# Transposing the columns of a recurrent step by DMA instead of by TensorE, and a softmax moved ahead, in a fused two-layer kernel

## The chip, the cores and the metric

The kernel runs on one core of a Trainium2 chip. The metric is the device time of one execution in microseconds (us), lower being better. Times shown are medians of several executions; a profile is one further execution with the hardware profiler on.

## What is computed

Two identical layers work on x, 2048 tokens of 448 values, in bf16. Each layer adds an attention part and then a gated feed-forward part.

```
x = x + A(layernorm(x));  x = x + B(layernorm(x))      # layer 1
x = x + A(layernorm(x));  x = x + B(layernorm(x))      # layer 2

A: mem = mem0                                   # 8 tokens
   for s in range(64):                          # segments of 32 tokens
       h = concat(mem, x[32s : 32s+32])         # 40 tokens
       q, k, v = h Wq, h Wk, h Wv               # 16 heads of 256
       p = softmax(mask(q k^T / 16))            # a token sees the 8 memory tokens and the tokens up to itself
       o = (p v) Wo
       mem, out[s] = o[:8], o[8:]               # the memory goes to the next segment
B: (relu(x Wgate) * (x Wup)) Wdown              # 448 -> 1792 -> 448
```

The loop over segments is a recurrence: segment s+1 can't begin until the 8 memory rows of segment s are there.

## The kernel before

**Folded weights.** At the start the kernel multiplies Wq with Wk^T and Wv with Wo for every head, so that a step needs neither keys nor values: scores come from h and a projected h (`A_sb`), and the output from the weighted rows of h itself, multiplied by `B_sb`. Heads are handled in two halves, called half 0 and half 1 (`hf`).

**Steps.** The main loop (line 1148) has 68 steps. Step g works on segment g of layer 1 and on segment g - 4 of layer 2 at once, so steps 4 to 63 have two layers ("two-layer steps", `two`), the first and last four have one. Every odd step from g = 3 on also carries a block of feed-forward work, `ff` (lines 545 to 682). I call these *long steps*, and the even ones *short steps*. In the two-layer stretch short and long steps alternate, 30 of each.

**A step's data.** The step's tokens stand as columns in `hT` (`hb[:, j, :]`): 448 features on partitions, in four chunks of 128 columns. VectorE and ScalarE write the new tokens' columns in `rows_in` (line 299, from the long step before), and VectorE writes the memory columns at the very end of the step before, in `project_last` (line 959) and in `finish` (line 967, the copy `hT<-ox`). The output needs the same tokens as rows too: 128 token slots on partitions, features along. This is `hk`, one of two buffers `HK[g % 2]` (line 525).

**How `hk` is made before.** `hk_make` (line 831) multiplies each of the four chunks of `hb` with the identity on TensorE, into one PSUM bank `kps`, and ScalarE copies that into `hk` in two pieces. `hk` is first read in `weigh_m(0, ...)`, then by `weigh_m(1, ...)` and `weigh_x`.

**Order within a step** (`step`, line 813). TensorE's instructions run in the order of the program text (`in_order`, line 84), and so do those of VectorE, ScalarE and of the DMA queue SP (`InOrder`, line 97). A step begins with `project(0, ...)`: half 0 of the projected h (`prj`), in five banks; after the second one `hk_make` stands. In long steps the residual and layer norm of the feed-forward block run on VectorE meanwhile, and `ff.fetch()` transposes the normed tokens (`xn`) into `xT`. Then `late` runs: `weigh_x(1, ...)` of the step before, which needs that step's half-1 weights `px1`. Then come half 1's projections, the scores of memory rows (`Sm`) and of ordinary rows (`Sx`), their softmaxes, and the output products (`ox`, `o`) by `project_out` and `project_last`.

**A softmax** (line 759) is four closures: `[3]` adds the mask, `[0]` takes the peak and subtracts it (VectorE), `[1]` is the exponential (ScalarE), `[2]` is sum, reciprocal and product (VectorE), which leaves the weights in `PX` (ordinary rows) or `PM` (memory rows). `m0`, `m1`, `x0`, `x1` are the softmaxes of memory and ordinary rows of half 0 and 1.

**How weights become columns.** Two ways exist. `flipped` transposes on TensorE (`pps`) and copies to `PT`. `fetched` (line 805) goes by DMA: SP writes `PX` to a scratch in DRAM (`dx`) and reads it back with a transposing DMA into `PT`; both are issued one after the other:

```
119  def turned(out, src, tag):
121      d = dram.tile([src.shape[0], src.shape[1]], BF, tag=f"d{tag}", name=f"d{tag}")
122      sp.dma_start(d[:], src)
123      sp.dma_start_transpose(out, d[:])
```

In two-layer steps a long step fetches `px0` and `px1`; a short step flips `px0` and fetches `px1` near its end. The read waits for the write to land, and whatever stands behind it on SP waits with it. `px1` is used by `weigh_x(1, ...)` early in the following step.

**SP's queue** in a pair of two-layer steps, before: short step `dx`, `PT` (half 1); long step `dxn`, `xT`, `dx`, `PT` (half 0), `dx`, `PT` (half 1), then four transfers of tokens (`xa<-xp`, `out_dram<-xa`, `xa<-in_A_x_dram`, `xp<-in_A_x_dram`).

Of the kernel before, what the change touches and what calls it, by code (L numbers as in the profile page):

```python
# [8 lines left out]
BF = mybir.dt.bfloat16  # L9
# [6 lines left out]
DM = 448  # L16
# [15 lines left out]
HI = 128  # L32
HW = 4 * HI
# [30 lines left out]
def build_kernel(ctx, tc, A_x, A_mem0, A_Wq, A_Wk, A_Wv, A_Wo, B_W_gate, B_W_up, B_W_down, out,  # L64
                 ntiles=16, nseg=64):
    nc = tc.nc
    P = nc.NUM_PARTITIONS
# [12 lines left out]
    dram = ctx.enter_context(tc.tile_pool(name="dram", bufs=2, space=bass.MemoryType.DRAM))  # L80
# [35 lines left out]

    dve, act, sp = InOrder(nc.vector), InOrder(nc.scalar), InOrder(nc.sync)

    def turned(out, src, tag):

        d = dram.tile([src.shape[0], src.shape[1]], BF, tag=f"d{tag}", name=f"d{tag}")
        sp.dma_start(d[:], src)
        sp.dma_start_transpose(out, d[:])

    now = [0]
    free_at = [0] * 8
# [3 lines left out]
    def bank(shape, dtype, name, after=700, hold=False):  # L130

        i = min((i for i in range(8) if i not in held), key=lambda i: free_at[i])
        t = psum.tile(shape, dtype, tag=f"b{i}", name=name)
        bank_of[t.name] = (i, after)
        free_at[i] = now[0] + 1000
        if hold:
            held.add(i)
        return t
# [25 lines left out]
    def evac(eng, dst, src):  # L164
        if eng is act:
            act.copy(dst, src)
        else:
            eng.tensor_copy(dst, src)
# [356 lines left out]
    HK = []  # L525
# [188 lines left out]
    def project(hf, chains, hb, j, banks, pre={}, busy=False, first=None, inside=None, head=0, between=None):  # L714

        n = L * len(chains)
        for i0, k in banks:
            ps = pre[i0] if i0 in pre else bank([P, 512], F32, "prj")
            two = len(chains) == 2

            def copies(eng, rows, T):
                if two:
                    evac(eng, T, ps[rows, 0:k * n].rearrange("p (t g q) -> p t g q", t=k, q=16))
                    return
                c = chains[0]
                src = ps[rows, 0:k * n].rearrange("p (t w) -> p t w", t=k)
                x, m = (0, SEG) if c == 0 else (MEM, 0)
                evac(eng, T[:, :, 2, MEM * c:MEM * c + MEM], src[:, :, m:m + MEM])
                evac(eng, T[:, :, 3 * c:3 * c + 2, :],
                     src[:, :, x:x + SEG].rearrange("p t (g q) -> p t g q", q=16))  # L730

            for i in range(k):
                if inside is not None and i == 4:
                    inside()
                if i0 not in pre:
                    tile_of(ps, hf, i0 + i, i, chains, hb, j, range(4), True, True)
                elif i >= head or i0 != banks[0][0]:
                    tile_of(ps, hf, i0 + i, i, chains, hb, j, range(3), False, True)
            if i0 in pre:
                let_go(ps)  # L740
            if first is not None:
                first()
            if between is not None:
                between()
            if i0 < 24:
                u0, eo = i0 // 12 * 6, i0 // 6 % 2
                T = TQ[hf][:].rearrange("p g u w -> p g (u w)").rearrange("p g (t e q) -> p t e g q", e=2, q=16)
                T = T[:, u0:u0 + 6, eo]
                copies(act if (i0 != 6 if busy and hf else i0 % 12) else dve, slice(0, P), T)
            else:  # L750
                for eng, e in ((act if busy else dve, 0), (act, 1)):
                    copies(eng, FR[e], TZ[hf][FR[e]].rearrange("p g (t e q) -> p t e g q", e=2, q=16)[:, :, e])
            if i0 in (6, 18):
                next_piece()
# [49 lines left out]

    def fetched(src, tag):
        PT = main.tile([P, 2, 128], BF, tag=f"PT{tag}", name="PT")
        turned(PT[:], src[:].rearrange("p b w -> p (b w)"), tag)
        return PT[:].rearrange("p b q -> p (b q)")

    def active(g):  # L810
# [2 lines left out]
    def step(g, ff, pre, late):  # L813
# [3 lines left out]
        gb, j = divmod(g, BLK)  # L817
        hb = hTb[gb % 2]
# [12 lines left out]
        def hk_make():  # L831
            kps = bank([P, 4, 128], F32, "kps")
            for i in range(4):
                n = 128 if i < 3 else 64
                mm(kps[:, i, 0:n], hb[:, j, i * HI:(i + 1) * HI], ident[:, 0:n], start=True, stop=True)
            hk = HK[g % 2]
            evac(act, hk[:].rearrange("p k n -> p (k n)")[:, 0:DM],
                 kps[:].rearrange("p k n -> p (k n)")[:, 0:DM])
            act.copy(hk[:, 4, 64:128], kps[:, 3, 0:64])
            return hk  # L840
# [46 lines left out]
        def weigh_m(hf, hk, PT):  # L887
            if not ms:
                return
            ya = bank([P, 256], F32, "ya")  # L890
            for kd in range(2):
                mm(ya[:, kd * 128:kd * 128 + 128], hk[:, kd, :], PT[:], start=True, stop=True)
            dve.tensor_copy(YB[hf][:, 0:16, M0:M0 + 16], ya[:].rearrange("p (t q) -> p t q", q=16))
            yb = bank([P, 192], F32, "yb")
            mm(yb[:, 0:128], hk[:, 2, :], PT[:], start=True, stop=True)
            for eo in range(2):
                mm(yb[:, 128:192], hk[:, 3 + eo, :], PT[:].rearrange("p (b o q) -> p b o q", o=2, q=16)[:, :, eo, :], start=(eo == 0), stop=(eo == 1))
            act.copy(YB[hf][:, 16:28, M0:M0 + 16], yb[:].rearrange("p (t q) -> p t q", q=16))
# [78 lines left out]
        def feed(*us):  # L977
            if ff is not None:
                for u in us:
                    ff.gate_up(u)  # L980


        two = len(chains) == 2
        early = ff is not None and two
        project(0, chains, hb, j, BANKS[0][0:1], pre, between=ff.residual if early else None)
        project(0, chains, hb, j, BANKS[0][1:2], pre)
        hk = hk_make()
        if ff is not None and not two:
            ff.residual()
        next_piece()  # L990
# [47 lines left out]
        m1, x1 = scores(1, True, True)  # L1038
# [24 lines left out]
        if ff is not None:  # L1063
            x1[3]()
            if len(chains) == 1:
                x0[0]()
                x1[0]()
            ox_open()
            mid = 18 if two else 10
            project_out(0, 0, mid)  # L1070
            ff.open_rows((0, 1, 2))
            if len(chains) == 2:
                x0[0]()
            x0[1]()
            m1[2]()
            x0[2]()
            if two:
                px0 = fetched(PX[0], "x0")
            feed(0)
            next_piece()  # L1080
            if len(chains) == 2:
                x1[0]()
            ff.products(1)
            ff.gated(1)
            pm = flipped(PM[1], 1, "m1", act) if ms else None
            x1[1]()
            ff.products(2)
            x1[2]()
            if two:
                px1 = fetched(PX[1], "x1")  # L1090
            else:
                px0 = flipped(PX[0], 2, "x0", act)
            weigh_m(1, hk, pm)
            ff.gated(2)
            feed(3)
            project_out(0, mid, mid + 8)
            next_piece()
            ff.down()
            ff.norm2()
            project_out(0, mid + 8, NT)  # L1100
            project_last()
            next_piece()
            project_out(1, 0, 12)
            if not two:
                px1 = flipped(PX[1], 2, "x1")
            fed = 20 if two else 18
            project_out(1, 12, fed)
            ff.feed_on()
            project_out(1, fed, NT)
        else:  # L1110
            next_piece()
            ox_open()
            m1[2]()
            x0[0]()
            x0[1]()
            late_flip = 23
            project_out(0, 0, late_flip)
            pm = flipped(PM[1], 1, "m1") if ms else None
            project_out(0, late_flip, NT)
            weigh_m(1, hk, pm)  # L1120
            x0[2]()
            x1[3]()
            x1[0]()
            x1[1]()
            x1[2]()
            if two:
                px1 = fetched(PX[1], "x1")
            next_piece()
            project_last()
            project_out(1, 0, 10)  # L1130
            px0 = flipped(PX[0], 2, "x0", act)
            project_out(1, 10, 25)
            if not two:
                px1 = flipped(PX[1], 2, "x1", act)
            next_piece()
            project_out(1, 25, NT)
# [11 lines left out]
    for g in range(nsteps):  # L1148
# [5 lines left out]
        i = (g - 3) // 2  # L1154
# [88 lines left out]
```

## Time and profile before

| | us |
|---|---|
| median of 3 runs | 1547.64 (1546.91 to 1550.41) |
| profiled execution, its own time | 1552.72 |
| span of the profile | 1550.9 |
| one short step, in the middle (801.20 to 818.95) | 17.75 |
| the long step after it (818.95 to 845.49) | 26.54 |
| copies `hk<-kps` on ScalarE, mean of one | 0.539 and 0.232 |
| writes `dx<-PX` and reads `PT<-dx` on SP | 90 of each |

In a line of the profile, L153 is the helper through which every matmul goes and L106 the one through which VectorE, ScalarE and SP go, so instructions are told apart by the names of their tiles. Names stand as output<-input. PE is TensorE's matmul, PEld its weight load, DVE VectorE, ACT ScalarE, POOL GpSimd, and SPq the queue SP on which DMAs are issued; the time in an SPq line is that of issuing, and a DMA's landing is listed apart. A timeline line has start, busy time, engine, instruction and, in brackets, the idle time before it and what ended that. Neighbouring matmuls overlap, so a group of them costs the distance from its start to the next group's start.

### The profile page before, as it was taken

Reading aid. Unit: us, or ns where it says so; the run is one execution under the profiler, and the core shown is the slowest. Engines: PE = TensorE matmul, PEld = TensorE weight load, DVE = VectorE, ACT = ScalarE, POOL = GpSimd, SP = SyncE. Lnnn points to the kernel's source line nnn. Section 1 sums busy time; section 2 is a strip of 40 time slices with the busy share of each in tenths; the row PEclk is TensorE's granted clock in tenths of the full one; section 3 lists DMA queues with packets and bytes.
Section 4 is the critical chain, followed back from the end, with each engine's and each line's share of the span. In section 5 each row is a group of like instructions: output and inputs, shape, how many; then the busy total and the mean of one; then the engine's idle time right before and its main releaser. Section 6 shows DMA issues by size and latency. Waiting matters only on the chain.

```text
span 1550.9 us, 89067 instructions
## 1 busy us (share of the span) xinstructions
PE 1533.7 (99%) x40635; PEld 1423.9 (92%) x40635; DVE 1092.4 (70%) x3591; ACT 744.3 (48%) x2059; POOL 77.6 (5%) x173
## 2 busy tenths in 40 slices
PE   9999999999999999999999999999999999999998
PEld 6689999999999999998999999999999999999997
DVE  7756777777777777776677777776767777767765
ACT  6744444454444444544454445444544544445444
POOL 3200000000000000000000000000000000000000
PEclk9999999999999999999999999999999999999999
DMA  8620011100100111000011101000011001000000
GB/s 254 204 65 11 20 27 26 25 22 22 25 20 23 27 26 25 22 22 24 18 25 27 26 21 23 24 22 23 24 27 27 21 22 25 20 22 24 23 7 10
DMA packets 88393, 52.22 MB, mean 34 GB/s; under 512 B 48008, under 2 KB 87120, under 8 KB 88016
## 3 DMA queue, kind: packets, MB, share of 16 engines
q1 hardware_dynamic: 85888, 42.33, 10.4%
q8 instruction: 318, 5.21, 1.4%
q0 software_dynamic: 1088, 3.68, 0.7%
q10 hardware_dynamic: 1040, 0.52, 0.1%
q14 instruction: 59, 0.48, 0.1%
HBM read 23.18 MB, written 11.60 MB: 22 GB/s over the span
## 4 chain that ended last, share of the span: by engine, by line
PE 96%; DMA 2%; DVE 1%; issue 0%; ACT 0%; POOL 0%; SPq 0%; DVEq 0%; ACTq 0%; POOLq 0%
PE prj L153 31%; PE ox L153 25%; PE gps L153 6%; PE ups L153 6%; PE dps L153 6%; PE o L153 5%; PE y L153 4%; PE Sx L153 3%; PE bps L153 1%; PE Sm L153 1%; PE ya L153 1%; PE aps L153 1%; PE yb L153 1%; PE tpw L161 1%; PE kps L153 1%; PE pps L161 1%
## 5 line engine op out<-in xcount | busy, mean ns | idle before, releaser
L153 PE MATMUL prj<-hT,A_sb 128*128 128x80 bf16 (+3 forms) x15232 | 551.8, 199 | 1.0 <-issue 0.6
L153 PEld LDWEIGHTS <-A_sb 128*128 128x128 bf16 (+1 forms) x15232 | 505.5, 99 | 21.2 <-issue 1.4
L153 PEld LDWEIGHTS <-B_sb 128*128 128x128 bf16 (+1 forms) x15008 | 484.7, 103 | 15.4 <-issue 2.4
L153 PE MATMUL ox<-Y,B_sb 128*128 128x80 bf16 (+2 forms) x11256 | 436.3, 200 | 1.9 <-issue 1.7
L106 ACT CAST TQ<-prj 128x480 bf16<-128x480 f32 (+1 forms) x380 | 184.5, 498 | 100.9 <-PE prj L153 87.7
L106 DVE CAST Y<-y 128x256 bf16<-128x256 f32 x376 | 151.3, 458 | 48.6 <-PE y L153 46.4
L106 ACT CAST Y<-y 128x512 bf16<-128x512 f32 (+2 forms) x392 | 137.0, 419 | 99.5 <-PE y L153 94.1
L106 ACT ACTIVATE se<-se 128x160 f32<-128x160 f32 (+2 forms) x270 | 81.6, 302 | 184.6 <-DVE se L106 176.1
L106 DVE CAST TQ<-prj 128x480 bf16<-128x480 f32 (+1 forms) x228 | 127.8, 569 | 15.7 <-PE prj L153 15.2
L153 PE MATMUL gps<-xT,Wg_sb 128*128 128x128 bf16 (+3 forms) x1904 | 128.7, 215 | 0.0
L106 DVE SCALAR_TENSOR_TENSOR hh<-gps,ut 128x512 bf16<-128x512 f32 (+2 forms) x136 | 78.1, 595 | 60.9 <-PE gps L153 37.8
L153 PEld LDWEIGHTS <-Wu_sb 128*128 128x128 bf16 (+1 forms) x1904 | 105.0, 97 | 5.7 <-issue 0.2
L153 PEld LDWEIGHTS <-hk 40*128 40x128 bf16 (+1 forms) x1950 | 98.8, 96 | 12.2 <-DMA PT<-dx 4.9
L153 PE MATMUL ups<-xT,Wu_sb 128*128 128x128 bf16 (+3 forms) x1632 | 107.0, 216 | 1.6 <-DMA xT<-dxn 1.2
L153 PEld LDWEIGHTS <-Wg_sb 128*128 128x128 bf16 (+1 forms) x1904 | 106.8, 97 | 1.6 <-issue 1.5
L106 DVE TENSOR_REDUCE ssum<-se 128x4 f32<-128x160 f32 (+2 forms) x270 | 73.4, 272 | 42.3 <-ACT se L106 38.5
L106 ACT CAST TZ<-prj 64x320 bf16<-64x320 f32 (+2 forms) x264 | 96.9, 377 | 8.4 <-DVE TZ L106 5.3
L106 ACT CAST ut<-ups 128x512 bf16<-128x512 f32 (+1 forms) x102 | 57.4, 563 | 81.1 <-PE ups L153 81.1
L106 ACT COPY os<-o 64x16 f32<-64x16 f32 (+3 forms) x134 | 25.6, 191 | 146.1 <-PE o L153 144.5
L153 PE MATMUL dps<-Wd_sb,hh 128*128 128x448 bf16 (+1 forms) x504 | 93.3, 342 | 0.8 <-DVE hh L106 0.8
L153 PE MATMUL y<-PT,hk 40*128 40x256 bf16 (+1 forms) x1280 | 86.0, 248 | 4.3 <-DMA PT<-dx 4.1
L106 DVE CAST Y<-ya 128x256 bf16<-128x256 f32 x134 | 56.9, 425 | 47.0 <-PE ya L153 46.5
(138 smaller groups left out, 1801.0 us busy)
## 6 DMA issues: line engine op xcount, KB each, us to landing
dx<-PX SPq DMA_DIRECT2D x90, 64.0 KB, 1.5
dxn<-xn SPq DMA_DIRECT2D x29, 128.0 KB, 1.7
wo<-in_A_Wo_dram POOLq DMA_DIRECT2D x8, 448.0 KB, 5.2
nat<-in_A_Wv_dram SPq DMA_DIRECT2D x8, 384.0 KB, 4.8
nat<-in_A_Wq_dram SPq DMA_DIRECT2D x6, 384.0 KB, 4.3
nat<-in_A_Wk_dram SPq DMA_DIRECT2D x6, 384.0 KB, 4.9
xa<-in_A_x_dram SPq DMA_DIRECT2D x32, 56.0 KB, 2.5
xa<-xp SPq DMA_DIRECT2D x32, 56.0 KB, 1.9
```

The costliest lines, as they stand in the source:

```text
L106: r = f(*a, **k)
L153: in_order(nc.tensor.matmul(out, lhsT, rhs, **k))
L161: in_order(nc.tensor.transpose(out, src, idn))
```

## The change

Two things change, both in two-layer steps only.

*The columns become rows by DMA.* At the head of the step, SP writes the step's columns (128 partitions, four chunks of 128) to a DRAM scratch `dh` of 512 rows of 128 values, one row for each feature, and two transposing DMAs read 448 and 64 of these rows into `hk`. The four matmuls into `kps` and ScalarE's two copies go away in these steps; one-layer steps keep `hk_make`. So that SP issues `dh` ahead of it, the transposing read of a fetched `PX` is no longer issued by `fetched` itself but kept in a list `to_read`, and issued by `read_rest`: in long steps at once, after a short step at the head of the next step, behind `dh`.

*Half 1's softmax of ordinary rows moves up in short steps.* The mask's addition `x1[3]` goes ahead of the first part of `project_out(0, ...)`, and peak, subtraction and exponential ahead of `x0[2]`, half 0's sum and product.

```diff
+    to_read = []
+
+    def sent(src, tag):
         d = dram.tile([src.shape[0], src.shape[1]], BF, tag=f"d{tag}", name=f"d{tag}")
         sp.dma_start(d[:], src)
-        sp.dma_start_transpose(out, d[:])
+        return d
+
+    def turned(out, src, tag):
+        sp.dma_start_transpose(out, sent(src, tag)[:])
+
+    def read_rest():
+        while to_read:
+            sp.dma_start_transpose(*to_read.pop(0))
...
     def fetched(src, tag):
         PT = main.tile([P, 2, 128], BF, tag=f"PT{tag}", name="PT")
-        turned(PT[:], src[:].rearrange("p b w -> p (b w)"), tag)
+        to_read.append((PT[:], sent(src[:].rearrange("p b w -> p (b w)"), tag)[:]))
...
         two = len(chains) == 2
         early = ff is not None and two
+        if two:
+            rows = dram.tile([HW, HI], BF, tag="dh", name="dh")
+            sp.dma_start(rows[:].rearrange("(i p) q -> p i q", p=P), hb[:, j, :].rearrange("p (i q) -> p i q", q=HI))
+        read_rest()
+        if two:
+            hk = HK[g % 2]
+            flat = hk[:].rearrange("p k n -> p (k n)")
+            sp.dma_start_transpose(flat[:, 0:DM].unsqueeze(1), rows[0:DM, :])
+            sp.dma_start_transpose(flat[:, 576:640].unsqueeze(1), rows[DM:HW, :])
         project(0, chains, hb, j, BANKS[0][0:1], pre, between=ff.residual if early else None)
         project(0, chains, hb, j, BANKS[0][1:2], pre)
-        hk = hk_make()
+        if not two:
+            hk = hk_make()
...
             if two:                                   # long step, after x0[2] and after x1[2]
                 px0 = fetched(PX[0], "x0")
+                read_rest()
...
             x0[1]()                                   # short step
+            if two:
+                x1[3]()
             late_flip = 23
             project_out(0, 0, late_flip)
             pm = flipped(PM[1], 1, "m1") if ms else None
             project_out(0, late_flip, NT)
             weigh_m(1, hk, pm)
+            if two:
+                x1[0]()
+                x1[1]()
             x0[2]()
-            x1[3]()
-            x1[0]()
-            x1[1]()
+            if not two:
+                x1[3]()
+                x1[0]()
+                x1[1]()
             x1[2]()
             if two:
                 px1 = fetched(PX[1], "x1")
```

More of the change, by code (lines that the diff above doesn't have):

```diff
@@ L117, in build_kernel @@
     dve, act, sp = InOrder(nc.vector), InOrder(nc.scalar), InOrder(nc.sync)
-    def turned(out, src, tag):
+    to_read = []
+    def sent(src, tag):
         d = dram.tile([src.shape[0], src.shape[1]], BF, tag=f"d{tag}", name=f"d{tag}")
         sp.dma_start(d[:], src)
-        sp.dma_start_transpose(out, d[:])
+        return d
[4 more added lines that the diff above has]
+            sp.dma_start_transpose(*to_read.pop(0))
     now = [0]
@@ L1090, in step @@
                 px1 = fetched(PX[1], "x1")
+                read_rest()
             else:
```

## The prediction

> **What bounds the kernel now.** First the page's busy line and its chain, to see which engine sets the end.
>
> ```profile
> span 1550.9 us, 89067 instructions
> PE 1533.7 (99%) x40635; PEld 1423.9 (92%) x40635; DVE 1092.4 (70%) x3591; ACT 744.3 (48%) x2059; POOL 77.6 (5%) x173
> PE 96%; DMA 2%; DVE 1%; issue 0%; ACT 0%; POOL 0%; SPq 0%; DVEq 0%; ACTq 0%; POOLq 0%
> ```
>
> TensorE is busy 99% of the span, and the chain that ended last runs through it for 96%. An average can hide a stage with another limit, so next the busy time by stage, for one short step (801.20 to 818.95) and the long step after it.
>
> ```profile
> 801.20:818.95 17.75, 17.75 (x528) 17.25 (x527) 12.85 (x45) 9.17 (x25) 0.00 (x0) 1.00 0.03 8
> 818.95:845.49 26.54, 26.54 (x660) 24.62 (x658) 18.82 (x59) 11.56 (x31) 1.58 (x4) 1.00 0.14 35
> ```
>
> The columns after the length are PE, PEld, DVE, ACT, POOL, granted clock and DMA share. PE fills both steps at full clock; VectorE is at 72% and 71%, ScalarE at 52% and 44%. So what leaves PE's stream leaves the time, unless a wait takes its place. What waits exist is in the list of waits; two rows matter here:
>
> ```profile
> PEld L153 <- DMA PT<-dx: 4.9, 4, 2.3
> PE y L153 <- DMA PT<-dx: 4.1, 3, 2.2
> ```
>
> PE already waits a few times for a transposed read. The PE timeline, read in windows over all steps, puts all four at one place: `weigh_x(1)` in a long step, at 288.79, 733.89, 1135.43 and 1269.72, with 0.3, 2.2, 0.6 and 1.3 us, **4.4 us** in all. That is the read this change delays.
>
> **What leaves: the four transposing matmuls.** Here is TensorE's timeline in the long step (start, us, instruction).
>
> ```profile
> 818.95 0.60 PE L153 MATMUL prj<-hT,A_sb 64*128 64x80 bf16 x24
> ...
> 821.49 0.36 PE L153 MATMUL kps<-ident,hT 128*128 128x128 bf16 x4
> 821.69 2.46 PE L153 MATMUL prj<-hT,A_sb 128*128 128x80 bf16 x67
> 823.98 0.61 PE L153 MATMUL y<-PT,hk 40*128 40x256 bf16 x10
> ```
>
> Matmuls overlap, so their cost is the distance between starts, not the 0.36 us: 821.69 - 821.49 = 0.20 us. The short step gives the same (803.52 to 803.72). Steps 4 to 63 have two layers: 60 x 0.20 = **12.0 us** off PE. In the instruction order nothing else of PE's stream moves; some PSUM banks change owner, which I cost at nothing: PE's steady steps show no idle time on a bank. ScalarE also loses two copies a step (539 + 232 ns); at 52% busy it sets no end, so 0.
>
> **What replaces them: SP's write of the columns and two transposing reads a step.** No row is the same transfer. The write `dh` is 128 KB in 512 pieces of 256 bytes. Nearest: `dxn<-xn`, 128 KB in 128 pieces, 1.7 us to landing and 0.34 us of SP; three-part loads (`nat`) hold SP 0.37 to 0.54. I take 0.45 us of SP. Pieces of 256 bytes are seen in the transposing reads: 288 packets at 9.7% of 16 engines in 3.0 us is 16 ns each, 544 packets of `xT<-dxn` 19 ns. So 512 pieces on 16 engines hold each for 32 x 0.019 = 0.6 us, and `dh` lands after some 2 us. A transposing read takes 1.2 us of SP (1.17 to 2.32) and lands after 2.3 to 5.0.
>
> When is `hk` due? First use is `weigh_m(0)`, at 828.48 in the long step and 810.43 in the short one. The last write into the step's columns is VectorE's `hT<-ox`:
>
> ```profile
> 819.06 0.21 DVE L106 CAST hT<-ox 128x48 bf16<-128x48 f32 x1 [0.40 <-PE ox L153]
> ```
>
> So `dh` issues at about 819.3 (short step: 801.5, SP's last transfer of the long step being issued by 801.2). It lands at 821.3, the two reads issue at 821.3 and 822.5, the second lands at 824.8 usually and 827.5 with the longest landing seen. With `kps` gone it is due 0.2 us sooner, so 0.8 us are left at the worst in the long step; in the short one it lands at 807.0, late at 809.7, against 810.2. I expect 0. If that cover went by 1 us everywhere it would cost 60 us.
>
> Behind these on SP stands `dxn` (VectorE ready at 824.3). SP is free again at 823.7, so usually no delay. With a late `dh` or reads that hold SP 2.3 us each, `xT` comes 1 to 2 us later; PE needs it at 831.3, it lands now after 2.4 to 5.0 from 826.1. Two waits of 0.5 and 0.7 us exist already. I take **+0.5 us** in all; bounds 0 and 5 (a quarter of 30 steps by 0.7).
>
> **What moves: the read of half 1's weights across the step's edge.** Before, `dx<-PX` was issued at 818.09 and its read 1.6 us later, at 819.69. Now this read stands behind `dh` on SP. On the other side, the short step's softmax of half 1 moves up on VectorE. Before, VectorE did, after `Y<-ya` (814.59 to 815.01): the sum, reciprocal and product of half 0, then add, peak and subtract of half 1, and then idled for the exponential:
>
> ```profile
> 817.17 0.32 DVE L106 TENSOR_REDUCE ssum<-se 128x4 f32<-128x160 f32 x1 [0.41 <-ACT se L106]
> ```
>
> After, the add falls into the gap before 813.94, and peak and subtract come ahead of half 0's sum: 814.93, 815.28, then half 0 from 815.53 to 816.42 (0.6 later; PE wants it at 816.7), half 1's sum at 816.34 and its `PX` at 817.24 instead of 818.06. So `dx` is issued 0.8 us sooner, at 817.3, and VectorE's 0.41 us gap closes. That gain doesn't reach the read, which now issues behind `dh` at 819.3 + 0.45 = 819.75 (or when `dx` has landed, if that is later). So the read starts 0.06 us later than in a typical step of before, and PE wants it 0.2 us sooner, since `kps` is gone.
>
> How long does it take? Asked one by one, these 30 reads land after 2.3 us in ten cases, up to 4.4 at most, 3.0 on average; the write ahead of them takes 1.6 us in half the cases and up to 3.8. Issue + landing + 0.05 gives the start of `y` in all four stalls (729.44 + 4.4 = 733.84). The same sum for the 30 steps of before gives 5.3 us of stalls against 4.4 seen, so I trust it to 1 us. For after I put max(`dx` landed, 819.75) + each case's own landing + c against 823.78, where c is the time that the read stands in the rings behind `dh`. Stalls over 30 steps, by c: 0 us 3.4, 0.3 us 5.5, 0.5 us 7.0, 0.7 us 9.3, 1.15 us 15, 1.9 us 32. `dh` moves from some 0.9 us after its issue for 0.6 us; the read follows 0.45 us behind: c = 0.15 to 0.6. I take 0.4: 6.2 us, **+1.5 us** on the 4.4 seen (against the sum's own 5.3 it would be 0.9). Bounds: -4.4 (all stalls go) and +28.
>
> No row of before shows a read that follows right behind a write, so c stays the widest term of the sum.
>
> **Sum.** -12.0 + 1.5 + 0.5 = -10.0 us. The profiled execution's 1552.7 goes to 1542.7. The runs shown have median 1547.6, 5.1 less; the change is the same per step, so **1537.6 us**.
>
> **Rivals.**
> 1. *`dh`'s small pieces cost double* and c is 1.15: 32 pieces at 2 x 25 ns (25 ns is what a piece of `dx`, 512 bytes, takes: 14% of 16 engines in 1.63 us over 144 packets) hold the rings 1.6 us. Stalls 15, net -12.0 + 10.7 + 0.5 = -0.8: 1546.8, no change. For it: no write to DRAM in pieces of 256 bytes is in the trace. Against it: 16 and 19 ns for the reads' pieces. Chance 0.10. [...]
> 2. *Slower: `dh` is paid by the piece*, and every long step waits in `weigh_x(1)`. `dx` lands in 1.5 us with 8 pieces an engine; if only 0.9 of that is fixed, a piece costs 75 ns, and 32 of them hold the rings 2.4 us: c = 1.9, stalls 32 us, net -12.0 + 27.6 + 0.5 = +16: 1564. It decides from c = 1.25 (stalls of 16). Against it: `dxn` with twice `dx`'s bytes in as many pieces lands 0.2 us later, so bytes count too. Chance 0.13.
> 3. *The full gain and no stalls*: c near 0, and the late writes of `dx` (up to 3.8 us), now begun 0.8 us sooner, no longer count: -12.0 - 4.4 = -16.4: 1531.2. Chance 0.10.
> 4. *The removal frees nothing*: PE then waits 0.2 us a step for the copies of `prj`. Against it: PE never waits for them now, and ScalarE loses work there. 1547.6. Chance 0.05.
>
> My own case, -6 to -14 us (1533.6 to 1541.6), has 0.62.
>
> **Range and chances.** A measurement of this kernel tells about 0.2% (3.1 us) from no change. Faster: 0.62 + 0.10, and 0.02 from rival 1's better end: 0.74. Same: 0.08 + 0.05 = 0.13. Slower: 0.13. The range 1531 to 1547 holds my case, rival 3 and rival 1 (0.82); rivals 2 and 4 lie outside.
>
> **What would show it.** Right: no `kps` in two-layer steps; starts of `prj` around its place 0.2 us closer; `dx` at the end of the short step 0.8 us sooner; `PT<-dx` in the long step right behind `dh`; a pair of steps 43.9 us instead of 44.3. Wrong: waits of `y` or its weights on `PT` well above 6 us (rivals 1, 2; the landing of `PT` behind `dh` gives c), waits of `ya` on `hk`, waits of `ups` on `xT` above 5 us, or PE idle on `prj` copies.

## The result, and the profile after

| | before | after |
|---|---|---|
| median of 9 runs, us | 1549.01 (1546.28 to 1550.77) | 1544.54 (1539.32 to 1546.10) |
| profiled execution, us | 1552.72 | 1544.96 |
| shortest pair of steps, us | 44.27 | 43.88 |
| `ups` waiting for `xT`, us | 1.2 | 9.6 |
| `y` waiting for `PT`, us | 4.1 | 1.1 |

The change makes the kernel faster by 4.5 us: the ratio is 0.997, with a 95% interval of 0.9958 to 0.9983. The forecast was 10 us, and the measured time lies inside the range given. The direction was right; the size was less than half. The time lies above my own case (1533.6 to 1541.6) and below rival 1 (1546.8), and neither mechanism made it: that it falls inside the range is luck.

The page of the kernel after, busy line and chain:

```profile
span 1543.1 us, 88881 instructions
PE 1520.7 (99%) x40395; PEld 1411.6 (91%) x40395; DVE 1087.2 (70%) x3591; ACT 712.4 (46%) x1939; POOL 77.4 (5%) x173
PE 92%; DMA 6%; DVE 1%; issue 0%; SPq 0%; POOL 0%; ACT 0%; DVEq 0%; POOLq 0%
PE prj L164 29%; PE ox L164 24%; PE gps L164 6%; PE ups L164 6%; PE dps L164 6%; PE o L164 5%; PE y L164 4%; PE Sx L164 3%; DMA xT<-dxn 3%; DMA dxn<-xn 2%; PE bps L164 1%; PE Sm L164 1%; PE ya L164 1%; PE tpw L172 1%; PE yb L164 1%; PE aps L164 1%
```

PE's busy time fell by 13.0 us, most of it the four matmuls. But PE's share of the chain fell from 96% to 92% and DMA's rose from 2% to 6%, and two names are new in the chain: `xT<-dxn` and `dxn<-xn`. The list of waits says who waits there (us in total, times, longest), the first line before, the others after:

```profile
PE ups L153 <- DMA xT<-dxn: 1.2, 2, 0.7
PE ups L164 <- DMA xT<-dxn: 9.6, 10, 1.7
PEld L164 <- DMA PT<-dx: 1.5, 3, 1.0
PE y L164 <- DMA PT<-dx: 1.1, 2, 0.9
```

The wait I watched, `y` on `PT`, shrank. The one to which I had added 0.5 us, `ups` on `xT`, is 9.6 us in ten of thirty long steps.

First PE in a long step, to see that the saving is there (the first line is of before, where `y` follows at 823.98):

```profile
820.63 0.39 PE L161 MATMUL otp<-ident,OT 128*128 128x128 bf16 x4
813.89 0.39 PE L172 MATMUL otp<-ident,OT 128*128 128x128 bf16 x4
814.12 3.10 PE L164 MATMUL prj<-hT,A_sb 128*128 128x80 bf16 x85
817.05 0.61 PE L164 MATMUL y<-PT,hk 40*128 40x256 bf16 x10
```

`kps` is gone and the projections run through: 817.05 - 813.89 = 3.16 us, against 823.98 - 820.63 = 3.35 before. Taken over the whole trace, a pair of steps that no wait disturbs took 44.27 or 44.28 us before and takes 43.88 or 43.89 after. That is 0.40 a pair, 12.0 us in 30 pairs.

Now the stages of the pair with that long step. Columns after the length as before: PE, PEld, DVE, ACT, POOL, granted clock, DMA share.

```profile
794.66:812.22 17.56, 17.56 (x526) 17.06 (x524) 12.68 (x45) 8.61 (x23) 0.00 (x0) 1.00 0.11 28
812.22:839.37 27.15, 26.40 (x656) 24.46 (x655) 18.81 (x59) 11.19 (x29) 1.58 (x4) 1.00 0.17 41
```

The short step is 0.19 shorter and full. In the long step PE is idle for 27.15 - 26.40 = 0.75 us. SP's timeline of this long step, with VectorE's last writes of `xn`, shows where it comes from (start, us of issuing or work):

```profile
812.55 0.38 SPq L106 DMA_DIRECT2D dh<-hT  x1
813.04 1.20 SPq L106 DMA_TRANSPOSE PT<-dx  x1
814.67 2.64 SPq L106 DMA_TRANSPOSE hk<-dh  x2
816.75 0.60 DVE L106 TENSOR_SCALAR xn<-xa,mv,rstd 128x448 bf16<-128x448 bf16 x2
817.38 0.55 SPq L106 DMA_DIRECT2D dxn<-xn  x1
821.09 1.21 SPq L106 DMA_TRANSPOSE xT<-dxn  x1
```

And PE's line at the wait:

```profile
825.10 0.21 PE L164 MATMUL ups<-xT,Wu_sb 64*128 64x128 bf16 x1 [0.75 <-DMA xT<-dxn]
```

SP was through with the two reads at 817.31, just ahead of `xn`, whose last write ends at 817.35, so `dxn` was issued in time here, at 817.38. (In 24 of the 30 long steps it was later than `xn` by over 0.1 us.) But its landing took 3.7 us; the shortest before was 1.7. The read `xT` could start only then, landed 4.0 us later, at 825.09, and PE went on at 825.10.

### The profile page after: what moved, and what is told of

Same layout as the page of the kernel before. It is cut to its first block, busy times and chain, and to the rows that moved or that the text cites. A ratio compares the mean times of both kernels' runs of the same rounds, so it can differ in the third digit from the quotient of the medians.

```text
span 1543.1 us, 88881 instructions
## 1 busy us (share of the span) xinstructions
PE 1520.7 (99%) x40395; PEld 1411.6 (91%) x40395; DVE 1087.2 (70%) x3591; ACT 712.4 (46%) x1939; POOL 77.4 (5%) x173
## 3 DMA queue, kind: packets, MB, share of 16 engines
q10 hardware_dynamic: 1040, 0.52, 0.1%
## 4 chain that ended last, share of the span: by engine, by line
PE 92%; DMA 6%; DVE 1%; issue 0%; SPq 0%; POOL 0%; ACT 0%; DVEq 0%; POOLq 0%
PE prj L164 29%; PE ox L164 24%; PE gps L164 6%; PE ups L164 6%; PE dps L164 6%; PE o L164 5%; PE y L164 4%; PE Sx L164 3%; DMA xT<-dxn 3%; DMA dxn<-xn 2%; PE bps L164 1%; PE Sm L164 1%; PE ya L164 1%; PE tpw L172 1%; PE yb L164 1%; PE aps L164 1%
## 5 line engine op out<-in xcount | busy, mean ns | idle before, releaser
L164 PE MATMUL prj<-hT,A_sb 128*128 128x80 bf16 (+3 forms) x15232 | 540.1, 199 | 0.3 <-ACT hT L106 0.3
L106 ACT COPY os<-o 64x16 f32<-64x16 f32 (+3 forms) x134 | 25.5, 190 | 146.1 <-PE o L164 144.5
```

Of the source, the lines that this page charges most:

```text
L106: r = f(*a, **k)
L164: in_order(nc.tensor.matmul(out, lhsT, rhs, **k))
```

## The experiments

**My theory after the result**: the 12 us are there, and some 8 of them go to `ups` waiting for `xT`, because the two reads into `hk` stand ahead of `dxn` and `xT`. **Rivals**: the write `dh` or DMA traffic in general slows every transfer; or the saving on PE counts little, and the softmax move brings what was gained. Each run was compared with the kernel before on its own chip, so ratios are to be compared. The median of before was 1549.0 us beside the full change, 1545.7 us beside e1 to e4 and 1546.9 us beside e5 to e7.

| run | median, us | ratio to before (95%) | `ups` on `xT`, us | shortest pair, us |
|---|---|---|---|---|
| full change | 1544.5 | 0.997 (0.9958 to 0.9983) | 9.6 | 43.88 |
| e1_short_only | 1541.5 | 0.9968 (0.9956 to 0.998) | 2.4 | 44.08 |
| e2_softmax_only | 1545.3 | 1.0 (0.9991 to 1.0008) | 1.4 | 44.27 |
| e3_rows_only | 1543.8 | 0.9981 (0.9968 to 0.9994) | 9.0 | 43.88 |
| e4_no_long_reads | 1533.9 | 0.9923 (0.991 to 0.9936) | 1.3 | 43.88 |
| e5_reads_twice | 1618.1 | 1.0438 (1.04 to 1.0476) | 62.6 | 44.73 |
| e6_one_read | 1534.5 | 0.9924 (0.991 to 0.9938) | 1.6 | 43.88 |
| e7_dxn_from_act | 1537.5 | 0.9941 (0.9929 to 0.9954) | 0.4 | 43.98 |

### e4: without the reads in long steps

```diff
-            sp.dma_start_transpose(flat[:, 0:DM].unsqueeze(1), rows[0:DM, :])
-            sp.dma_start_transpose(flat[:, 576:640].unsqueeze(1), rows[DM:HW, :])
+            if ff is None:
+                sp.dma_start_transpose(flat[:, 0:DM].unsqueeze(1), rows[0:DM, :])
+                sp.dma_start_transpose(flat[:, 576:640].unsqueeze(1), rows[DM:HW, :])
```

> As the full change, but the two reads into hk are left out in long steps (hk keeps old values there, so the output product of long steps uses wrong rows); the write dh stays. Theory (the reads are what delays xT): dxn lands in 1.7 us again, waits of ups on xT fall to 1 to 2 us, time 10 to 12 us below before. Rival (the write dh, or the late read of PX, is what delays xT): waits on xT stay near 9 us and the time stays near the full change.

Measured: ratio 0.9923, 11.8 us below before, and waits on `xT` of 1.3 us. SP in a long step of this run:

```profile
807.19 0.38 SPq L106 DMA_DIRECT2D dh<-hT  x1
807.68 1.22 SPq L106 DMA_TRANSPOSE PT<-dx  x1
812.01 0.34 SPq L106 DMA_DIRECT2D dxn<-xn  x1
813.70 1.24 SPq L106 DMA_TRANSPOSE xT<-dxn  x1
```

`dxn` lands 1.7 us after its issue again, so the read starts at 813.70. The write `dh` and the late read of `PX` are still there and cost nothing that shows. The rival falls; the two reads are the cause of the late `xT`.

### e5: the reads doubled

```diff
             sp.dma_start_transpose(flat[:, 576:640].unsqueeze(1), rows[DM:HW, :])
+            if ff is not None:
+                spare = main.tile([P, 5, 128], BF, tag="spare", name="spare", bufs=2)
+                sflat = spare[:].rearrange("p k n -> p (k n)")
+                sp.dma_start_transpose(sflat[:, 0:DM].unsqueeze(1), rows[0:DM, :])
+                sp.dma_start_transpose(sflat[:, 576:640].unsqueeze(1), rows[DM:HW, :])
```

> As the full change, but in long steps the two reads of the rows are issued a second time, into a spare tile. Theory (time on SP and in the rings ahead of dxn and xT sets the stalls): dxn is issued some 2.4 us later, xT arrives 2.4 us later, and nearly every long step waits in ups for about 2 us: 45 to 75 us of waits in place of 9.6, time 1580 to 1610. Rival (the stalls come from a few unlucky collisions that don't grow with the queue): waits of 10 to 20 us, time 1545 to 1555.

Measured: all thirty long steps wait, 62.6 us in all.

```profile
PE ups L164 <- DMA xT<-dxn: 62.6, 30, 3.5
```

From the start of a long step's `otp` (the transposes that open it), `xT` arrives after 12.3 us in the median, against 10.0 in the full change. That is 2.3 us later, close to the 2.4 us expected. More reads brought more waits (62.6 us against 9.6), so a few unlucky collisions are not the cause. The time is above the range expected, 1618 in the median (1607 to 1634) against 1580 to 1610, and this is a miss with a cause of its own. Here are a wait, the stretch after it and the one after that (the granted clock stands third from the end):

```profile
1096.00:1099.75 3.75, 0.67 (x19) 0.62 (x16) 1.56 (x8) 0.34 (x1) 0.00 (x0) 0.87 0.21 49
1099.75:1105.40 5.65, 5.62 (x64) 5.42 (x64) 1.24 (x3) 0.75 (x2) 0.00 (x0) 0.50 0.08 18
1105.40:1111.00 5.60, 5.60 (x90) 4.81 (x88) 2.81 (x7) 2.10 (x6) 0.00 (x0) 0.98 0.09 23
```

After the 3.1 us wait the clock is granted at half for 5.65 us. Thirteen of the thirty waits are followed by such a stretch. Half of PE's busy time in these stretches, summed, is 25.5 us lost; with 61 us more waits than e4 that makes 87 of the 88 us between the two spans (1620.2 and 1532.2).

### e6: one read instead of two

The 64 rows of the second read repeat 64 rows of the first, so a copy on GpSimd within `hk` can take its place.

```diff
-            sp.dma_start_transpose(flat[:, 576:640].unsqueeze(1), rows[DM:HW, :])
...
             if two:
                 ff.fetch()
+        if two:
+            nc.gpsimd.tensor_copy(hk[:, 4, 64:128], hk[:, 3, 0:64])
```

> As the full change, but the second read (64 rows, which repeat 64 rows of the first) is replaced by a copy on GpSimd within hk. SP is free 1.2 us sooner, before xn is ready. Theory: dxn is issued as soon as xn is there (0.4 us sooner than in the full change), lands in about 1.9 us, waits of ups on xT fall from 9.6 to 2 to 4 us, time 1536 to 1539 against before at 1546 to 1549. Rival (the bytes of the first read are what blocks, not the number of reads): waits of 6 to 9 us, time as the full change.

Measured: ratio 0.9924, 11.8 us below before by it. This beats both kernels. SP in a long step:

```profile
810.74 1.15 SPq L106 DMA_TRANSPOSE hk<-dh  x1
811.98 0.53 SPq L106 DMA_DIRECT2D dxn<-xn  x1
```

and the copy with its engine's wait, out of the views of `hk` and of the waits:

```profile
L1017 POOL COPY hk<-hk x60: 237/238/293, 138.5 to 1428.2; 128x64 bf16<-128x64 bf16 x60
```

```profile
POOL hk L1017 <- DMA hk<-dh: 211.2, 45, 10.1
PE ups L164 <- DMA xT<-dxn: 1.6, 2, 0.9
```

SP is through with the read before `xn` is ready, so `dxn` is issued 3.49 us after `otp` in the median (3.96 in the full change) and lands in 1.7 us (2.3). GpSimd waits 211 us for the reads, and no cost of that shows. The rival, with waits of 6 to 9 us, falls. The waits on `xT` are below what I expected, 1.6 against 2 to 4 us, and the time with them.

### e7: `dxn` issued from ScalarE's queue

```diff
-            turned(xT[:, :, self.n], self.xn[self.n, :], "xn")
+            d = dram.tile([P, 512], BF, tag="dxn", name="dxn")
+            act.dma_start(d[self.n, :], self.xn[self.n, :])
+            sp.dma_start_transpose(xT[:, :, self.n], d[self.n, :])
```

> As the full change, but dxn is issued from ScalarE's queue, so it no longer waits for SP to issue the two reads; the read xT stays on SP. This splits the delay into SP's issue time and time in the rings. If SP's issue time counts: dxn is issued 0.4 us sooner, waits on xT fall by a third to a half, time 2 to 4 us below the full change. If the rings count alone: dxn is issued sooner but lands as late as before, waits stay near 9 us, time within 1 us of the full change.

Measured: ratio 0.9941, waits on `xT` of 0.4 us, fewer than in any other run. So both expectations were too low: `dxn` doesn't wait for SP to issue the reads, and it lands 0.4 us sooner after its issue. The DMA issues of this run, then of the full change (KB each, median us to landing):

```profile
dxn<-xn ACTq DMA_DIRECT2D x29, 128.0 KB, 1.9
xT<-dxn SPq DMA_TRANSPOSE x30, 2.7
```

```profile
dxn<-xn SPq DMA_DIRECT2D x29, 128.0 KB, 2.3
xT<-dxn SPq DMA_TRANSPOSE x30, 3.5
```

`dxn` lands in 1.9 us instead of 2.3, with the same reads issued (`hk<-dh` lands in 3.0 and 3.1 us). Its packets are listed in another queue: q10 has 5296 packets in this run and 1040 in the full change, q1 147872 and 152128. By the medians the run is 2.9 us slower than e6 all the same (the two intervals overlap a little): its shortest pair is 0.10 us longer, 3 us over 30, and `y` waits 2.5 us for `PT`. I didn't try to separate the two; that ScalarE, which now stops for `xn`, makes the 0.10 us is only argued.

### e1: rows by DMA in short steps alone

```diff
+        by_dma = two and ff is None
-        if two:
+        if by_dma:
...
-        if not two:
+        if not by_dma:
             hk = hk_make()
```

> Rows by DMA in short steps only; long steps keep the four matmuls, so no read of hk stands ahead of dxn and xT. Theory (the gain of 12 us is there, and some 8 of it go to waits of ups on xT, because the two hk reads of a long step stand ahead of dxn and xT): half of the PE gain stays, an undisturbed pair of steps is 44.08 us, waits of ups on xT fall from 9.6 to 1 to 2 us, and the time is 5 to 8 us below before (ratio 0.995 to 0.9965), so no worse than the full change. Rival (more DMA traffic slows every transfer, wherever it stands): waits on xT stay at 4 to 5 us, and the time is 2 to 3 us below before.

Measured: pairs of 44.08 us as expected, waits on `xT` of 2.4 us, no wait of `y` on `PT`, and 4.2 us below before by the medians (4.9 by the ratio), a little less than the 5 to 8 expected. The waits lie above the 1 to 2 us of the theory and well below the rival's 4 to 5. Half the DMA work gives as much as all of it, since the other half pays for itself with waits.

### e2 and e3: each half of the change alone

> Only the softmax moves up in short steps; rows come from the four matmuls as before. The write of PX should be issued 0.8 us sooner and its read with it. Theory: PE loses no work, pairs stay at 44.28 us, and only the stalls of y on PT go: 1 to 4 us below before. Rival (the softmax move is where the whole measured gain comes from): 4 to 5 us below before.

> Rows by DMA in all two-layer steps, softmax order as before. Theory: the read of PX is held by dh and not by PX's write, so it starts at the same time as in the full change: waits on xT some 9 us, waits of y on PT 1 to 4 us, time within 3 us of the full change. Rival (the softmax move carries the gain): as slow as before.

e2 takes the two hunks of the softmax in short steps onto the kernel before; e3 leaves these two out of the kernel after. Measured: e2 has the ratio 1.0 (0.9991 to 1.0008), less than the 1 to 4 us expected and than the rival's 4 to 5. Its read `PT` is sooner and `y` never waits for it in its trace, but the time is the same, so the kernel before can lose little to that wait in most executions. e3 has 0.9981, beside 0.997 for the full change, and the intervals overlap. Its waits:

```profile
PE ups L164 <- DMA xT<-dxn: 9.0, 8, 2.0
PEld L164 <- DMA PT<-dx: 3.4, 3, 1.8
PE y L164 <- DMA PT<-dx: 2.9, 2, 1.7
```

The waits on `xT` are those of the full change; `y` waits 2.9 us for `PT` instead of 1.1. The read of `PX` didn't start quite as in the full change, as I had expected: it was issued 0.86 us behind `dh` on average, against 0.62. The softmax move shows no gain alone; beside the DMAs the two ratios differ by some 1.7 us, which is within the noise, so these runs can't tell.

## Why the prediction was right or wrong, step by step

**The four matmuls (-12.0 us): right.** 44.28 to 43.88 us per undisturbed pair is 0.40, 12.0 in all. Rival 4, that the removal frees nothing, is refuted.

**`hk` in time (0): right.** No matmul of `weigh_m` or `weigh_x` waits for `hk` in the lists of waits. `dh` lands after 2.1 us in the median (2.0 at best), where I had some 2. The two reads together hold SP 2.9 us on average, where I had 2.4.

**The moved read (+1.5): wrong in sign, harmlessly.** VectorE's order came out as worked out: `PX` is ready 2.06 us ahead of `dh`'s issue (median from `dx` to `dh`), and the read follows `dh` by 0.49 us. The thirty reads land after 3.09 us on average behind `dh`, against 3.05 before, so c, the widest term of my sum, is near 0. Rivals 1 and 2, which needed 1.15 us or more, are refuted: the pieces of 256 bytes didn't hold up the read that follows. The doubled piece of rival 1 shows in no run: in the trace's packet records one such piece of `dh` takes 17 ns on average, not the 50 of rival 1 or the 75 of rival 2. Rival 3 had this part right, c near 0 and most stalls on `PT` gone, but not the waits on `xT`. `dh` lands 0.4 us later than `dxn` before (2.1 against 1.7 us), which has as many bytes in larger pieces; what makes the 0.4 us, no run here shows.

The profiled execution of before also flattered this term. Its longest wait for `PT`, 2.2 us, brought 1.7 us of lower clock with it: the pair with it took 48.17 us, 3.89 more than its neighbours. So `PT` cost 6.1 us in that execution (the 4.4 of the prediction and this 1.7), which stood 3.7 us above the later median. e2 shows that a usual execution loses little there.

**What stands behind on SP (+0.5, bounds 0 and 5): this is the step that failed.** It came to +8.4 us (9.6 after, 1.2 before), above its upper bound. I asked only when SP is free again and answered 823.7, before `xn` at 824.3, "so usually no delay". The runs put three things in its place. From the start of a long step's `otp`, means over 29 steps, and medians in the last row:

| us | before | after | e4 (reads left out) |
|---|---|---|---|
| `dxn` issued | 3.69 | 3.96 | 3.49 |
| its landing | 1.94 | 2.54 | 1.97 |
| `xT` read issued | 5.64 | 6.52 | 5.47 |
| its landing | 3.20 | 3.48 | 3.11 |
| `xT` there | 8.84 | 10.00 | 8.58 |
| PE wants it (median) | 10.59 | 10.39 | 10.39 |

SP is late, since in long steps `dh` lands after 2.2 us on average, not 2.0, and the reads hold SP 2.9 us, not 2.4: `dxn` could go at 3.49 now, and goes 0.47 later. It then stands behind the two reads: in the packet records its first packet starts 1.32 us after its issue on average, against 0.84 before, and in no long step ahead of the reads' last packets. To its landing it takes 0.60 us more. I had worked out just this delay, c, for the read behind `dh`, and not for `dxn` behind the reads of `hk`. And the next landing is 0.28 longer. With PE's 0.2 us the slack fell from 1.75 to 0.39 us, while single landings spread over 2 us (`dxn` 1.9 to 4.0, `xT` 2.4 to 4.4). The sum that I had made for `PT` tells it here too: the 30 arrivals of `xT` before, held against PE's 10.39, give 1.6 us of waits with no delay, 0.4 more than before and close to my +0.5, and 7.4 us with each arrival 1.16 us later, as it was on average. (This is an estimate; 9.6 were measured.) The prediction named this risk in its bounds, and took it to need a late `dh` or reads that hold SP 2.3 us each.

**The sum.** In the profiled executions: -12.0 by the matmuls, +8.4 by `xT`, -5.0 by `PT` with its clock (6.1 to 1.1) is -8.6; the two differ by -7.8. Between the medians it is -4.5: there, by e2, nearly all that `PT` seemed to give is missing, and -12.0 + 8.4 = -3.6 is left. That is an estimate, since the 8.4 comes from one execution of each kernel.

## What to carry to other kernels

The DMAs that moved onto SP were paid for twice here by what stands behind them: `dxn` was issued 0.47 us later than it could have been, and took 0.60 us more from issue to landing. So work out the slack of each later transfer down to the instruction that waits for it, and against the spread of landings, not their median. When a gain on the bounding engine is smaller than expected, compare undisturbed steps first: here they showed the full 0.40 us, which left only the waits to be searched, and one read fewer gave them back.

## What the runs showed that I had not expected

A short idle time of TensorE cost more than itself here. In the trace of e5 waits up to 1.83 us left the granted clock at 1.00 each time; from 1.89 us up, thirteen waits of fifteen were followed by a clock of 0.50, most for some 3.4 us (1.7 us lost), three for longer (2.9 us lost), while waits of 2.12 and 2.94 us were not. The kernel before did it once, after 2.19 us:

```profile
731.00:734.00 3.00, 0.81 (x25) 0.61 (x23) 0.84 (x3) 0.72 (x2) 0.00 (x0) 1.00 0.19 57
734.00:739.00 5.00, 5.00 (x101) 4.85 (x98) 3.17 (x10) 2.70 (x8) 0.00 (x0) 0.66 0.12 26
```

The granted clock of before is 0.50 for 3.41 us, from 734.43 to 737.84. In e5 the half-clock stretches begin a whole number of times 3.413 us apart (at 255.66, 303.45 and 351.24, each 14 times that after the last). Cut into stretches of 3.413 us by this, the trace has 1.89 us or more of idle PE in the stretch ahead of each of the thirteen, and at most 1.87 in any that full clock followed. The wait of 2.94 us lay across the end of one stretch and the start of the next (PE's busy time stands first after the length):

```profile
204.47:207.88 3.41, 1.56 (x44) 1.52 (x41) 2.42 (x11) 0.61 (x2) 0.00 (x0) 1.00 0.08 18
207.88:211.30 3.42, 2.33 (x52) 2.22 (x52) 0.00 (x0) 0.58 (x1) 0.00 (x0) 1.00 0.28 67
```

That is 1.85 and 1.09 us idle. In e3 a stretch with 1.9 us of idle time passed, so these traces part at some 1.9 us in one stretch, and no sharper.
